# Half-head blocks with 64 KB rows in a decode attention kernel that streams K and V

## The chip, the cores and the metric

The kernel runs on one core of a Trainium2 chip. The metric is device time in microseconds (us), the median of several executions. All runs told here were classed as fast (no execution over 1.5% above the fastest of its kernel); executions of one kernel agree within about 0.3%, and medians of several of them closer, so differences of half a per cent can be told apart when kernels are timed in the same rounds on the same chip.

## The reference

One query token, 32 query heads, 8 K/V heads, 65536 keys, head size 128, all in bf16. Each K/V head serves four query heads.

```python
B, Hq, Hkv, Sq, Sk, D = 1, 32, 8, 1, 65536, 128
scores = jnp.einsum("bhqd,bhkd->bhqk", q, k) * D ** -0.5
p = softmax(scores, axis=-1)
return jnp.einsum("bhqk,bhkd->bhqd", p, v)
```

K and V are 134 MB each. Every byte is read once, so the kernel is a stream of 268.44 MB through the core.

## The kernel before

A K/V head is cut into C = 4 blocks of 16384 keys. A block is 4 MB of K and 4 MB of V. Partition p takes 128 keys that lie next to each other, so one partition's row of a transfer is 32 KB. There are three K buffers and two V buffers.

```python
T = 128                 # keys per partition in a block
TG = 16                 # keys per partition in a group: one transpose
U = 2                   # score units in a block, one PSUM bank each
NK, NV = 3, 2           # K and V buffers
NKT = 4                 # buffers of transposed K
...
def load_k(i):
    if i >= NK:
        sp.wait_ge(tr_s, (i - NK + 1) * G)      # block i-3 is transposed
    ...
    sp.dma_start(kbuf[i % NK][:, :], src(kf, i)).then_inc(k_in[i % NK], 16)

def load_v(i):
    if i >= NV:
        sp.wait_ge(pv_s, i - NV + 1)            # block i-2 is multiplied
    ...
for j in range(N + LAG):                        # LAG = 5: V trails K by a head
    if j < N:
        load_k(j)
    if j >= LAG:
        load_v(j - LAG)
```

SyncE issues the loads in this order. VectorE (DVE) transposes each group of K in 32x32 blocks. TensorE (PE) multiplies the transposed K with the spread query into PSUM (`scores`). ScalarE (ACT) copies the scores to SBUF in 32x64 pieces, 16 of them per unit. When all four blocks of a head have scores, GpSimd takes the maximum over partitions, ACT takes exponentials, and PE multiplies them with V (`values`), four columns per key row. The last V block is loaded in small pieces to shorten the end.

```python
def move(u):                                    # ACT: one unit of scores, PSUM to SBUF
    ...
    for x in range(A):
        for a in range(A):                      # A = 4: 16 small copies
            ins = ac.activation(to[a * S4:(a + 1) * S4, x, :, :],
                                fr[x * S4:(x + 1) * S4, a, :, :], AF.Copy)
```

## Time and profile before

| before | value |
|---|---|
| time | 638.81 us (median of 4) |
| profiled span, first to last instruction | 636.8 us |
| bytes read / mean rate over the span | 268.47 MB / 422 GB/s |
| busiest engine | DVE, 53% |

These are lines of the page of before: the span, the busy time of each engine, then the span in 40 slices with the busy tenths of the DMA engines and their rate, the packet counts, and the chain of work that ended last. q1 is the queue on which K and V come, q8 and q14 bring instructions.

```profile
span 636.8 us, 20414 instructions
PE 325.1 (51%) x8197; PEld 294.2 (46%) x8197; DVE 334.7 (53%) x379; ACT 290.8 (46%) x1291; POOL 7.2 (1%) x25
...
DMA  9999999999999999999999999999999999999995
GB/s 369 436 422 441 431 428 428 430 431 430 434 434 439 430 427 427 430 432 434 431 434 436 432 427 428 430 430 435 420 430 432 422 428 418 434 429 385 389 423 246
...
q1 hardware_dynamic: 10656, 268.44, 98.6%
q8 instruction: 5, 0.08, 0.1%
q10 hardware_dynamic: 368, 0.04, 0.0%
q14 instruction: 13, 0.11, 0.0%
...
DMA 66%; DVE 20%; PE 10%; issue 2%; ACT 1%; SPq 1%; ACTq 0%
```

The DMA engines are busy in every slice until the last; no compute engine is above 53%. The kernel waits for its bytes.

The windows view of before, by stage (start and end, length, busy time and instructions of five engines, clock, DMA share, GB/s), shows the weak place at the end:

```profile
30.00:300.00 270.00, 141.87 (x3418) 126.61 (x3419) 161.64 (x173) 138.19 (x620) 2.77 (x7) 1.00 1.00 431
300.00:560.00 260.00, 131.88 (x3454) 120.97 (x3450) 140.16 (x157) 117.73 (x525) 2.40 (x6) 1.00 1.00 428
560.00:600.00 40.00, 22.88 (x640) 21.24 (x639) 15.85 (x23) 21.89 (x96) 0.82 (x2) 1.00 0.99 408
```

The trace also lists every DMA packet with its start, duration and size. One packet of the K/V queue is one partition's row. The median durations of before are:

| row | 2 KB | 4 KB | 8 KB | 16 KB | 32 KB |
|---|---|---|---|---|---|
| ns | 84 | 159 | 309 | 611 | 1213 to 1215 |

They lie on a straight line: about 9 ns, plus 27.2 GB/s per engine, which is 435 GB/s on 16 engines. The Trainium skill ("DMA: Bandwidth & Descriptors", Where 436 GB/s comes from) gives the same figure, 435.2 GB/s, as the ceiling of the ports on the SBUF side, and this trace agrees. All the bytes at 435 GB/s on 16 engines take 617.1 us.

### The profile page before, as it was taken

How to read it: one execution, taken by the hardware profiler on the slowest of the kernel's cores; microseconds unless marked ns; L12 is line 12 of the kernel's file. 1: busy time of each engine (PE TensorE's matmuls, PEld its weight loads, DVE VectorE, ACT ScalarE, POOL GpSimd, SP SyncE). 2: the span in 40 equal slices, each digit the busy share in tenths (PEclk: the TensorE clock that was granted, in tenths of full speed). 3: DMA queues.
4: the chain of work that ended last, by engine and by line, in shares of the span. 5: the costliest groups of instructions: out<-in, count | busy, mean ns of one | idle time of the engine just before them, and what ended most of it. 6: DMA issues, size and time to landing. Idle time of an engine off the chain costs nothing.

```text
span 636.8 us, 20414 instructions
## 1 busy us (share of the span) xinstructions
PE 325.1 (51%) x8197; PEld 294.2 (46%) x8197; DVE 334.7 (53%) x379; ACT 290.8 (46%) x1291; POOL 7.2 (1%) x25
## 2 busy tenths in 40 slices
PE   2466764345653456634466434665345654385346
PEld 1355554335552345533455433554334553375335
DVE  5599865445664446654466534566344664482000
ACT  1466854355433554335553345533355434466120
POOL 0000000000000000000000000000000000000000
DMA  9999999999999999999999999999999999999995
GB/s 369 436 422 441 431 428 428 430 431 430 434 434 439 430 427 427 430 432 434 431 434 436 432 427 428 430 430 435 420 430 432 422 428 418 434 429 385 389 423 246
DMA packets 11042, 268.67 MB, mean 422 GB/s; under 512 B 1552, under 2 KB 1552, under 8 KB 2192
## 3 DMA queue, kind: packets, MB, share of 16 engines
q1 hardware_dynamic: 10656, 268.44, 98.6%
q8 instruction: 5, 0.08, 0.1%
q10 hardware_dynamic: 368, 0.04, 0.0%
q14 instruction: 13, 0.11, 0.0%
HBM read 268.47 MB, written 0.01 MB: 422 GB/s over the span
## 4 chain that ended last, share of the span: by engine, by line
DMA 66%; DVE 20%; PE 10%; issue 2%; ACT 1%; SPq 1%; ACTq 0%
DMA kbuf<-in_k_dram 59%; DVE ktb L278 18%; DMA vbuf<-in_v_dram 7%; PE qkb L178 5%; PE acc L189 4%; DVE hpart L286 2%; ACT scs L371 1%; SPq L135 1%; PE row L240 0%; SPq L125 0%; SPq L138 0%; PE row L246 0%; ACT olast L408 0%; DVE hmax L293 0%; PE acc L235 0%
## 5 line engine op out<-in xcount | busy, mean ns | idle before, releaser
L278 DVE STREAM_TRANSPOSE ktb<-kbuf 128x1024 int32<-128x1024 int32 x256 | 298.5, 1214 | 220.3 <-DMA kbuf<-in_k_dram 219.9
L178 PE MATMUL qkb<-qblk,ktb 128*128 x4096 | 224.6, 178 | 278.2 <-DVE ktb L278 268.1
L371 ACT ACTIVATE scs<-qkb 32x64 f32<-32x64 f32 x1024 | 219.5, 214 | 297.8 <-PE qkb L178 286.6
L178 PEld LDWEIGHTS qkb<-qblk,ktb 128*128 128x128 bf16 x4096 | 187.2, 105 | 305.3 <-issue 287.1
L189 PE MATMUL acc<-pts,vbuf 128*128 128x4 bf16 x4080 | 142.3, 166 | 31.3 <-DMA vbuf<-in_v_dram 29.9
L189 PEld LDWEIGHTS acc<-pts,vbuf 128*128 128x128 bf16 x4080 | 128.0, 104 | 34.5 <-DMA vbuf<-in_v_dram 29.4
L388 ACT ACTIVATE pts<-scs,negb 128x128 bf16<-128x128 f32 x128 | 66.9, 570 | 28.5 <-PE acc L189 27.7
L286 DVE TENSOR_REDUCE hpart<-scs 128x4 f32<-128x256 f32 x64 | 36.4, 569 | 5.8 <-ACT scs L371 5.8
L388 ACT ACTIVATION_READ_ACCUMULATOR pts<-scs,negb 128x1 f32 x128 | 23.9, 187 | 0.0
L309 DVE TENSOR_TENSOR o<-acc,o 128x4 f32<-128x4 f32 x8 | 1.3, 162 | 38.0 <-PE acc L189 25.1
L306 DVE COPY o<-acc 128x4 f32<-128x4 f32 x8 | 1.3, 161 | 27.8 <-PE acc L189 27.8
L163 POOL PARTITION_ALL_REDUCE hmaxa<-hmax x8 | 3.0, 371 | 574.4 <-DVE hmax L293 574.4
L408 ACT ACTIVATE olast<-row,rrow 4x128 bf16<-4x128 f32 x1 | 0.4, 358 | 15.4 <-PE row L240 15.4
L167 POOL PARTITION_ALL_REDUCE lsum<-rsum x7 | 3.6, 511 | 0.9 <-ACT pts L388 0.9
L360 ACT ACT_TABLE_LOAD x1 | 1.3, 1283 | 2.7 <-issue 2.7
L240 PE MATMUL row<-vbuf,pts 128*4 128x128 bf16 x16 | 2.1, 308 | 0.0
L293 DVE TENSOR_REDUCE hmax<-hpart 128x4 f32<-128x32 f32 x8 | 1.7, 210 | 0.3
L240 PEld LDWEIGHTS row<-vbuf,pts 128*4 128x4 bf16 x16 | 1.6, 122 | 0.2
L379 ACT ACTIVATE negb<-hmaxa 128x4 f32<-128x4 f32 x8 | 1.6, 203 | 0.2
L256 DVE STREAM_TRANSPOSE qt<-q 128x64 int32<-128x64 int32 x1 | 0.2, 245 | 2.5 <-DMA q<-in_q_dram 2.5
L317 DVE RECIPROCAL recip<-lhead 128x4 f32<-128x4 f32 x7 | 1.2, 178 | 0.2
L321 DVE TENSOR_TENSOR oT<-o,recip 128x4 bf16<-128x4 f32 x7 | 1.1, 163 | 0.2
(24 smaller groups left out, 6.9 us busy)
## 6 DMA issues: line engine op xcount, KB each, us to landing
vbuf<-in_v_dram SPq DMA_DIRECT2D x31, 4096.0 KB, 17.4
kbuf<-in_k_dram SPq DMA_DIRECT2D x30, 4096.0 KB, 26.8
kbuf<-in_k_dram SPq DMA_DIRECT2D x5, 1024.0 KB, 22.2
kbuf<-in_k_dram SPq DMA_DIRECT2D x1, 2048.0 KB, 11.2
vbuf<-in_v_dram SPq DMA_DIRECT2D x1, 2048.0 KB, 10.3
kbuf<-in_k_dram SPq DMA_DIRECT2D x2, 512.0 KB, 4.3
vbuf<-in_v_dram SPq DMA_DIRECT2D x1, 1024.0 KB, 12.5
vbuf<-in_v_dram SPq DMA_DIRECT2D x1, 512.0 KB, 13.2
```

The costliest lines, as they stand in the source:

```text
L135: sp.dma_start(vbuf[i % NV][:, :], src(vf, i)).then_inc(v_in[i % NV], 16)
L163: g.partition_all_reduce(hmaxa[:, hs], hmax[:, hs], P, bass.bass_isa.ReduceOp.max).then_inc(hma_s, 1)
L167: g.partition_all_reduce(lsum[:, ps], rsum[:, ps], P, bass.bass_isa.ReduceOp.add).then_inc(ls_s, 1)
L178: ins = pe.matmul(qkb[(e * U + g // GU) % NQ][:, at:at + A * R], lhsT=kt[:, be // NE, be % NE, n * P:(n + 1) * P], rhs=qblk[:, bass.ds(col ...
L189: ins = pe.matmul(acc[:, 0:R], lhsT=vbuf[e][:, t * D:(t + 1) * D], rhs=pts[e][:, t * R:(t + 1) * R], start=e == 0 and t == 0, stop=e == E ...
L240: ins = pe.matmul(row[0:R, 0:D], lhsT=pts[E - 1][:, t * R:(t + 1) * R], rhs=vbuf[E - 1][:, t * D:(t + 1) * D], start=t == T - TG, stop=t = ...
L278: dv.transpose(to.rearrange("p (b t j) -> p b t j", b=NB, t=TG), fr.rearrange("p (t b i) -> p b t i", b=NB, t=TG),).then_inc(tr_s, 1)
L286: dv.tensor_reduce(hp[:, h % 2, c, :], scs[h % 2][:, c * W:(c + 1) * W].rearrange("p (n g) -> p g n", g=R), AX.X, ALU.max,).then_inc(mx_s, 1)
L293: dv.tensor_reduce(hmax[:, h * R:(h + 1) * R], hp[:, h % 2, :, :].rearrange("p u g -> p g u"), AX.X, ALU.max,).then_inc(hm_s, 1)
L371: ins = ac.activation(to[a * S4:(a + 1) * S4, x, :, :], fr[x * S4:(x + 1) * S4, a, :, :], AF.Copy)
L379: ac.activation(negb[:, hs], hmaxa[:, hs], AF.Copy, scale=-scale).then_inc(nb_s, 1)
L388: ac.activation(pv[:, g_, :], sv[:, g_, :], AF.Exp, bias=negb[:, col], scale=scale, accum_out=rsum[:, i * R + g_:i * R + g_ + 1],).then_in ...
```

## The change

The intent is fewer and longer rows. A head is now cut into C = 2 blocks of 32768 keys; a partition's row is 64 KB and a transfer is 8 MB. Two K buffers and one V buffer of 8 MB take 192 KB of each SBUF partition, where the five buffers of before took 160; to make room, the buffers of transposed K fall from four to two, and the small tensors are packed into one. The score buffer now holds one block instead of two heads, so the softmax runs with a maximum that is corrected at the second block: the first block's sums and outputs are multiplied by exp(first maximum - total maximum). The last two V blocks are loaded in halves, each as soon as PE has done the same half of the block before.

```diff
-T = 128
+T = 256
-U = 2
+U = 4
-NK, NV = 3, 2
-NKT = 4
+NK = 2
+NKT = 2
-KLAST = (32, 32, 32, 32)
+KLAST = (64, 64, 64, 64)
+HALVED = 2
...
         def load_v(i):
-            if i >= NV:
-                sp.wait_ge(pv_s, i - NV + 1)
+            if i < N - HALVED:
+                if i >= 1:
+                    sp.wait_ge(pv_s, 2 * i)
+                load(vbuf, vf, i, 0, T, v_in)
+                return
+            sp.wait_ge(pv_s, 2 * i - 1)
+            load(vbuf, vf, i, 0, TH, va_in)
+            sp.wait_ge(pv_s, 2 * i)
...
-        for j in range(N + LAG):
+        load_k(0)
+        for j in range(1, N + 1):
             if j < N:
                 load_k(j)
-            if j >= LAG:
-                load_v(j - LAG)
+            load_v(j - 1)
...
+        def weigh(h):
+            ...
+            dv.tensor_tensor(o2, o1, wgt, ALU.mult).then_inc(ow_s, 1)
+            ...
         def exponent(i):
...
+            if b:
+                ac.activation(wgt, dif, AF.Exp, scale=scale).then_inc(wg_s, 1)
```

PE's loop now does all 16 groups of `scores` of block j and then all `values` of block j-1, where before it did them group by group in turn. The waits cut from `weigh` and `exponent` above are in the kernel.

## The prediction

> **What bounds the kernel now.** The transfers. The page's DMA row is 9 in every slice but the last; the HBM line gives 422 GB/s over the 636.8 us span. No engine is over 53% busy (DVE 334.7 us). The chain of waits is 66% DMA. Windows by stage: 431 GB/s in 30–300 us, 428 in 300–560, but 408 in 560–600.
>
> In the trace's list of DMA packets one packet is one partition's row; median times are 84, 159, 309, 611, 1213 ns for 2, 4, 8, 16, 32 KB: a straight line, about 8.5 ns fixed plus 27.2 GB/s per engine, 435 GB/s on 16. The Trainium skill ("DMA: Bandwidth & Descriptors", Where 436 GB/s comes from) states the same ceiling, 435.2; this trace agrees. The bytes alone need 617 us. The other 20 us of the span (an estimate, from the packets): 2.75 before the first packet, 5.3 fixed packet cost (9472 rows x 9 ns / 16), 0.7 completions, 5 of packets slower than their median, 3.4 after the last packet, 3 of under-filled engines in the V-only tail, where a V load waits for PE to free one of two buffers.
>
> **What the change does.**
> - 5760 data rows instead of 9472, 45 transfers instead of 74. Saves 3712 x 9 / 16 = 2.1 us plus 0.3 for completions, if a 64 KB row is one packet; nothing if it is cut in two.
> - One K buffer, one V buffer and two of four transposed-K buffers go. A V load now waits for all value matmuls of the block before, which PE does after the next block's scores. From K_j landing (t = 0; an 8 MB transfer is 19.5 us): 16 transposes at 1.22 us (1.13 back to back, plus waits for two buffers) plus two maxima at 0.5: scores end near 22. V_{j-1} landed at 19.5; values, 256 x 34 ns = 8.7, end at 31; V_j is issued then, while K_{j+1} fills the engines to 39. Slack 8 us against 2.0 from an issue to its first packet: no bubble.
> - Exponentials (256 wide, under 1 us each) run near 31–36; the running maximum adds about six operations of 0.2 us per head. Off the critical path: DVE works 33 of 39 us per block.
> - Tail: DVE stands in `collect` for block 13 until 31 after K_14 landed, transposes block 15 until 54; values(14) follow, so V_15's first half is issued near 59, just after V_14 landed (58.5): one bubble of 2–3 us, in place of the 3 us lost now.
>
> **Predicted time.** 638.85 − 2.4 (packets) − 0.5 (tail) − 0.3 (fewer slow packets) = 635.7 us. Range 631 to 641. Faster by over 2%: 0.01 (bytes plus start and end alone are about 625). Within 2%: 0.93. Slower: 0.06.
>
> **What would show each step.** 64 KB packets of about 2419 ns and about 6480 packets on the K/V queue (10000 mean the rows are cut); middle slices of 431–434 GB/s; DVE still waiting for K several us per block; SyncE waiting for PE before V loads with K in flight; one dip below 400 GB/s where the last V starts.
>
> **What would make it wrong.** Bubbles in every block, if transposes, scores and values take over 37 us from K's landing (each lost us costs 15 in all). A 64 KB pitch slower in HBM: the same page (Latency and other measured facts) reports slower copies at large power-of-two pitches, such as 2 MiB; no run here shows it. More slow packets.

## More of the kernel before

The costliest groups of instructions of before (line, engine, operation, tiles, count, then busy us, mean ns, and the idle time before them with its cause):

```profile
L278 DVE STREAM_TRANSPOSE ktb<-kbuf 128x1024 int32<-128x1024 int32 x256 | 298.5, 1214 | 220.3 <-DMA kbuf<-in_k_dram 219.9
...
L371 ACT ACTIVATE scs<-qkb 32x64 f32<-32x64 f32 x1024 | 219.5, 214 | 297.8 <-PE qkb L178 286.6
```

DVE stands idle for 220 us waiting for K.

## The result, and the profile after

| | before | after |
|---|---|---|
| time, median of 4 | 638.81 us | 636.12 us |
| span of the profiled run | 636.8 us | 634.0 us |
| data rows / transfers of K and V | 9472 / 74 | 5760 / 45 |
| first packet to last packet, from the first instruction | 1.73 to 632.40 us | 1.72 to 629.72 us |

The ratio of after to before is 0.9957, 95% interval 0.9939 to 0.9974. A ratio is the mean time of one kernel's fast runs over that of the other's of the same rounds, so it is not quite the ratio of the medians in the tables. The predicted time was 635.7 us, in a range of 631 to 641.

The same parts of the page of after:

```profile
span 634.0 us, 18764 instructions
PE 271.7 (43%) x8197; PEld 245.2 (39%) x8197; DVE 341.0 (54%) x411; ACT 276.2 (44%) x1179; POOL 10.3 (2%) x33
...
DMA  9999999999999999999999999999999999999995
GB/s 365 429 450 418 443 430 435 438 426 438 422 447 426 438 426 435 438 422 447 418 455 418 442 431 426 442 422 443 422 455 410 451 426 434 430 410 437 430 359 219
...
q1 hardware_dynamic: 6480, 268.44, 98.4%
q8 instruction: 5, 0.08, 0.1%
q14 instruction: 14, 0.11, 0.0%
...
DMA 48%; DVE 27%; PE 15%; another core or an unknown queue 9%; issue 1%; SPq 1%; POOL 0%; ACT 0%; ACTq 0%
```

The queue carries 6480 packets: 5760 rows and 45 x 16 completions, as predicted. A 64 KB row is one packet, median 2421 ns (the line gives 2419). The slices swing more because one packet is now 2.4 us; the windows view of after gives the rates that can be compared:

```profile
30.00:300.00 270.00, 116.23 (x3498) 104.54 (x3499) 153.48 (x178) 125.65 (x541) 3.90 (x10) 1.00 1.00 432
300.00:560.00 260.00, 110.02 (x3359) 99.59 (x3357) 137.73 (x163) 110.94 (x473) 3.90 (x10) 1.00 1.00 434
560.00:600.00 40.00, 22.18 (x658) 19.74 (x659) 31.80 (x38) 24.77 (x109) 0.80 (x2) 1.00 0.98 420
```

The groups of after that answer to those of before:

```profile
L284 DVE STREAM_TRANSPOSE ktb<-kbuf 128x1024 int32<-128x1024 int32 x256 | 295.8, 1213 | 161.2 <-DMA kbuf<-in_k_dram 158.2
L375 ACT ACTIVATE scs<-qkb 32x64 f32<-32x64 f32 x1024 | 220.5, 215 | 281.3 <-PE qkb L184 270.1
```

DVE still waits for K, 158 us, in every block. The timeline of after around a block in the middle (start, length, what):

```profile
433.81 10.38 DVE L284 STREAM_TRANSPOSE ktb<-kbuf 128x1024 int32<-128x1024 int32 x9 [10.91 <-DMA kbuf<-in_k_dram]
...
453.84 6.98 PE L195 MATMUL acc<-pts,vbuf 128*128 128x4 bf16 x256
...
460.85 0.33 SPq L119 DMA_DIRECT2D vbuf<-in_v_dram  x1
...
472.51 8.16 DVE L284 STREAM_TRANSPOSE ktb<-kbuf 128x1024 int32<-128x1024 int32 x7 [11.49 <-DMA kbuf<-in_k_dram]
```

K lands at 433.81, `values` of the block before end at 460.8, the next V is issued 27.0 us after the landing, and the next K lands 38.7 us after it. The issue comes 11.7 us before the K transfer ahead of it is done, so the engines do not run dry. This is the main wait that the change could have lost to, and it costs nothing.

So far the prediction stands. Two things did not fit. First, the tail of after still has under-filled slices; in slices of 2 us they are 355 and 280 GB/s at 602 to 606 us and 298 twice at 614 to 618 us. Second, the packets that are slower than their median are not spread evenly, and most follow an 8 KB packet on the instruction queue. The experiments take the row length first and then these two.

A correction for what follows: the prediction and the first texts place packets on an axis that begins 1.0 to 1.3 us before the first instruction. In this section and in all tables the axis begins at the first instruction, as in the profile's views. The prediction's "2.75 before the first packet" and "3.4 after the last packet" are 1.73 and 4.4 us on it, with the same sum, and its "2.0 from an issue to its first packet" is about 1.0 us (before: issue at 577.93, first packet at 578.91).

### The profile page after: what moved, and what is told of

The parts are those of the page before. It is cut to its first block, busy times and chain, and to the rows that moved or that the text cites. A ratio compares the mean times of both kernels' runs of the same rounds, so it can differ in the third digit from the quotient of the medians.

```text
span 634.0 us, 18764 instructions
## 1 busy us (share of the span) xinstructions
PE 271.7 (43%) x8197; PEld 245.2 (39%) x8197; DVE 341.0 (54%) x411; ACT 276.2 (44%) x1179; POOL 10.3 (2%) x33
## 3 DMA queue, kind: packets, MB, share of 16 engines
q1 hardware_dynamic: 6480, 268.44, 98.4%
## 4 chain that ended last, share of the span: by engine, by line
DMA 48%; DVE 27%; PE 15%; another core or an unknown queue 9%; issue 1%; SPq 1%; POOL 0%; ACT 0%; ACTq 0%
DMA kbuf<-in_k_dram 30%; DVE ktb L284 25%; DMA vbuf<-in_v_dram 17%; PE acc L195 13%; PE qkb L184 2%; DVE small L291 1%; SPq L119 1%; PE row L248 0%; POOL small L165 0%; PE row L254 0%; DVE small L335 0%; ACT ktb L408 0%; DVE small L317 0%; DVE small L313 0%
## 5 line engine op out<-in xcount | busy, mean ns | idle before, releaser
L284 DVE STREAM_TRANSPOSE ktb<-kbuf 128x1024 int32<-128x1024 int32 x256 | 295.8, 1213 | 161.2 <-DMA kbuf<-in_k_dram 158.2
L184 PE MATMUL qkb<-qblk,ktb 128*128 x4096 | 157.3, 176 | 343.0 <-DVE ktb L284 330.3
L184 PEld LDWEIGHTS qkb<-qblk,ktb 128*128 128x128 bf16 x4096 | 132.9, 105 | 367.2 <-issue 199.0
L195 PE MATMUL acc<-pts,vbuf 128*128 128x4 bf16 x4080 | 112.0, 166 | 17.2 <-DMA vbuf<-in_v_dram 16.7
L195 PEld LDWEIGHTS acc<-pts,vbuf 128*128 128x128 bf16 x4080 | 110.4, 104 | 18.9 <-DMA vbuf<-in_v_dram 15.1
L291 DVE TENSOR_REDUCE small<-scs 128x4 f32<-128x256 f32 x64 | 38.0, 593 | 61.4 <-ACT scs L375 61.4
L392 ACT ACTIVATE pts<-scs,small 128x256 bf16<-128x256 f32 x64 | 48.9, 852 | 34.8 <-PE acc L195 34.8
L160 POOL PARTITION_ALL_REDUCE small<-small x16 | 6.0, 372 | 574.8 <-DVE small L302 574.8
L392 ACT ACTIVATION_READ_ACCUMULATOR pts<-scs,small 128x1 f32 x64 | 13.6, 212 | 0.0
L381 ACT ACTIVATE small<-small 128x4 f32<-128x4 f32 x16 | 3.3, 205 | 21.8 <-POOL small L160 21.8
L313 DVE TENSOR_TENSOR small<-small 128x4 f32<-128x4 f32 x8 | 1.3, 163 | 18.1 <-PE acc L195 18.1
L307 DVE TENSOR_TENSOR small<-small 128x4 f32<-128x4 f32 x8 | 1.3, 164 | 4.0 <-POOL small L160 4.0
L165 POOL PARTITION_ALL_REDUCE small<-small x7 | 3.0, 432 | 18.5 <-DVE small L317 18.5
L315 DVE TENSOR_TENSOR small<-small 128x4 f32<-128x4 f32 x8 | 1.3, 156 | 2.7 <-ACT pts L392 2.7
```

Source lines behind the costliest of these rows:

```text
L160: g.partition_all_reduce(mtot if b else mfirst, hmax[:, b * R:(b + 1) * R], P, bass.bass_isa.ReduceOp.max,).then_inc(hma_s, 1)
L165: g.partition_all_reduce(lsum, rhead, P, bass.bass_isa.ReduceOp.add).then_inc(ls_s, 1)
L184: ins = pe.matmul(qkb[g // GU][:, at:at + A * R], lhsT=kt[:, be // NE, be % NE, n * P:(n + 1) * P], rhs=qblk[:, bass.ds(qcols[be], A * R)] ...
L195: ins = pe.matmul(acc[:, 0:R], lhsT=vbuf[:, t * D:(t + 1) * D], rhs=pts[:, t * R:(t + 1) * R], start=t == 0, stop=t == T - 1,)
L284: dv.transpose(to.rearrange("p (b t j) -> p b t j", b=NB, t=TG), fr.rearrange("p (t b i) -> p b t i", b=NB, t=TG),).then_inc(tr_s, 1)
L291: dv.tensor_reduce(hp[j % C][:, u * R:(u + 1) * R], scs[:, u * W:(u + 1) * W].rearrange("p (n g) -> p g n", g=R), AX.X, ALU.max,).then_inc ...
```

## The experiments

Twelve kernels ran; all gave correct outputs. The kernel before was timed in the same rounds each time; its medians were 638.5 to 638.8 us. before_wide and the three busy runs ran on another chip than the rest, so times of different rounds are best compared through the ratio.

| run | time, us | ratio to before, 95% interval |
|---|---|---|
| rows_32k | 638.63 | 0.9996 (0.9983 to 1.001) |
| rows_16k | 642.58 | 1.0058 (1.0044 to 1.0072) |
| quarter_tail | 636.03 | 0.9958 (0.9944 to 0.9972) |
| late_collect | 636.23 | 0.9959 (0.9945 to 0.9973) |
| act_nops | 639.20 | 1.001 (0.9996 to 1.0023) |
| dve_nops | 637.59 | 0.9984 (0.9971 to 0.9998) |
| wide | 633.11 | 0.9917 (0.9903 to 0.9931) |
| wide_quarter | 633.26 | 0.9918 (0.9904 to 0.9931) |
| before_wide | 635.38 | 0.9952 (0.9938 to 0.9965) |
| busy_256 | 652.85 | 1.0212 (1.0195 to 1.0228) |
| busy_384 | 738.17 | 1.156 (1.1542 to 1.1578) |
| busy_mid | 642.44 | 1.0062 (1.005 to 1.0074) |

### Is the gain the fixed cost of a packet? rows_32k and rows_16k

The changed kernel, with each whole 8 MB transfer cut into CUT = 2 or 4 transfers of shorter rows. Nothing else changes.

```diff
-                load(kbuf[i % NK], kf, i, 0, T, k_in[i % NK])
+                for c in range(CUT):
+                    load(kbuf[i % NK], kf, i, c * T // CUT, (c + 1) * T // CUT, k_in[i % NK])
...
-            dv.wait_ge(k_in[j % NK], 16 * (j // NK + (j % NK > 0)))
+            dv.wait_ge(k_in[j % NK], 16 * CUT * (j // NK + (j % NK > 0)))
```

V is cut in the same way.

> The changed kernel with each of its 28 whole 8 MB transfers cut into two of 32 KB rows; buffers, waits and softmax as changed. Theory A (the gain is the fixed 8.5 to 9 ns of a packet): 3584 more rows and 28 more transfers cost 3584 x 9 / 16 + 28 x 9 = 2.3 us, so 638.4 us, median 32 KB packet 1213 ns, about 10500 packets on the queue. Rival B (the gain comes from the rest of the change: other waits, fewer slow packets): the time stays within 0.3 us of the changed kernel, 636.1 us.

> The same with four transfers of 16 KB rows. Theory A: three times as much, 6.0 + 0.8 = 6.8 us, so 642.9 us, median 16 KB packet 611 ns. Rival B: still 636 to 637 us.

Measured: 638.63 and 642.58 us, against 638.4 and 642.9 expected for theory A. The median packets were 1218 and 613 ns. The queue counts follow: 6480 packets in after, these in rows_32k and then rows_16k (lines of their pages).

```profile
q1 hardware_dynamic: 10512, 268.44, 98.5%
```

```profile
q1 hardware_dynamic: 18576, 268.44, 98.7%
```

With 32 KB rows the changed kernel takes the time of the kernel before. So the whole gain is the row length, and the rest of the change, with fewer buffers, another order of loads and another softmax, is neutral in sum. Rival B fell. (A cut adds transfers as well as rows, in a fixed proportion, so these runs do not part the cost of the two; the packet durations do: two rows of 32 KB take 2 x 1213 = 2426 ns, one of 64 KB 2418 to 2421.)

### Does the tail cost anything? quarter_tail and late_collect

In after, the tail runs like this (timeline; the first half of V_14 lands, PE multiplies it, only then may the first half of V_15 be issued):

```profile
599.94 3.57 PE L195 MATMUL acc<-pts,vbuf 128*128 128x4 bf16 x128 [0.83 <-DMA vbuf<-in_v_dram]
...
609.64 3.57 PE L195 MATMUL acc<-pts,vbuf 128*128 128x4 bf16 x128 [6.12 <-DMA vbuf<-in_v_dram]
```

PE ends the first half at 603.5. Yet the fastest DMA engine has nothing left to do from 602.96, where its part of V_14 ends. quarter_tail loads the last two V blocks in quarters, so that more is in flight:

```diff
-            sp.wait_ge(pv_s, 2 * i - 1)
-            load(vbuf, vf, i, 0, TH, va_in)
-            sp.wait_ge(pv_s, 2 * i)
+            for c in range(4):
+                sp.wait_ge(pv_s, 4 * (i - 1) + c + 1)
+                if i < N - 1 or c < 2:
+                    load(vbuf, vf, i, c * TQ, (c + 1) * TQ, vq_in[c])
+                    continue
```

late_collect keeps the halves and moves only DVE's collection of block 13 into the middle of block 15's transposes:

```diff
+                if j == N - 1 and g == G // 2 - 1:
+                    collect(N - 3)
...
-            if j >= 1:
+            if j >= 1 and j != N - 2:
                 collect(j - 1)
```

> The changed kernel with the last two V blocks loaded in quarters instead of halves, each issued as soon as PE has done the same quarter of the block before. Theory C (the tail starves because with halves the loop of [...]values 3.6, issue to first packet 2.1, plus 2 to 3 us spread between the 16 DMA engines, is longer than the 9.7 us a half takes): the loop shrinks to 6 + spread against 14.5 us of transfers in flight, both dips (273 and 331 GB/s near 604 to 608 us, 227 near 616) go, and the time falls by 2 to 2.8 us to 633.3 to 634.1 us. Rival D (the tail waits for DVE, which stands in the collection of block 13 before it transposes block 15, as the prediction had it): the first quarter of the last V goes out about 2.7 us earlier at best, the first dip shrinks, the second stays, gain about 1 us or less.

> The changed kernel with only the collection of block 13 moved from before to the middle of block 15's transposes, so that DVE starts on block 15 several us earlier; V in halves as changed. Theory C: no change (within 0.3 us of 636.1), because the first half of V_14 lands 0.8 us after PE is ready for it and stays the limit. Rival D: the dip near 604 us goes, 634 to 635 us.

Measured: 636.03 and 636.23 us, no gain from either. late_collect speaks against the prediction's reason for the dip (DVE standing in `collect`). quarter_tail is the surprise: it did what it should to the transfers and nothing to the time. In slices of 2 us the rate stays at 420 GB/s or more until 622 us; both dips are gone. But the last packet ends at 629.87 us, as in after (629.72). The rate only falls earlier: 339, 133, 43 and 24 GB/s in the four slices from 622 us. Most of the 16 DMA engines are done by about 624 us and wait for one.

Theory C thus described the dips rightly and their cost wrongly. (On the corrected axis its loop is 0.5 us from the last packet of a landing to PE's start, 3.6 of values, 1.0 from the issue to the first packet, and a spread of 6.2 us, 593.25 to 599.44, on the first half of V_14.) The fast engines were idle in the tail, but the last engine was not: it ended the halves of V_14 at 599.44 and 609.14 us, and the first half of V_15 had been issued at 603.55.

### One DMA engine sets the pace

Every engine writes one 4-byte completion packet per transfer, so the 16 completions of a transfer show when the first and the last engine were done with it. On transfers of after (the first row is a 4 MB piece of the first block, the others are whole; times in us):

| the first engine ended a transfer at | last engine | spread | instruction fetches of 8 KB since the row above |
|---|---|---|---|
| 22.18 | 24.50 | 2.33 | none |
| 41.50 | 44.86 | 3.36 | 36.7 (309 ns); also two of 16 KB at 39.2 and 39.5 |
| 351.10 | 354.57 | 3.47 | six, at 73.3 to 293.4 |
| 370.45 | 374.60 | 4.15 | 366.7 (309 ns) |
| 409.15 | 413.31 | 4.16 | none |
| 428.50 | 433.33 | 4.83 | 425.4 (309 ns), 428.4 (325 ns) |
| 467.20 | 472.04 | 4.84 | none |
| 486.55 | 492.07 | 5.52 | 489.0 (309 ns) |
| 544.60 | 550.11 | 5.51 | none |

The spread grows in steps of 0.67 to 0.69 us, and a step falls where an 8 KB packet of 309 ns stands on q14. The packet list shows the cost of one: at 489.0 us the fetch takes 309 ns on an engine, and the 64 KB row after it takes 2798 ns in place of 2421. That is 0.31 + 0.38 = 0.69 us. The Trainium skill ("DMA: Bandwidth & Descriptors", Queues, rings and completion order) says that row 14 of the queues is the runtime's own, for refills among others; these packets fit that. Nine fetches of 309 to 318 ns come, 51 to 76 us apart, and one more of 707 ns in the tail, at 617.8 us. The trace records 1226 ACT instructions, waits included (the expectations below count 1292); at 64 bytes each (the skill's "Runtime: NRT & Kernel Launch", Instruction fetch mechanics, counts 256 instructions to 16 KiB) 8 KB are 128 of them, which makes about 10 fetches, an estimate that act_nops checks below. A rarer kind of 325 ns, followed by a row of 3080 ns (1.0 us together), comes four times and would be DVE's, with 461 instructions recorded.

The packets carry no engine number. But on one engine a packet starts 3 to 4 ns before the recorded end of the last one, so the packets can be chained, which is a reconstruction and not a record. In it all nine fetches of the first kind lie on one engine and all four of 325 ns on another. The first of these engines lags 0.75 us behind the fastest near 61 us, 3.47 near 296 us and 5.52 near 492 us. That is why the fetches from 73 to 293 us hardly moved the spread: until then a third engine was last, 3.39 us behind, and the engine with the 309 ns fetches had yet to catch up with it.

This gives theory E: one DMA engine brings ACT's instructions besides its share of K and V, falls behind by 0.69 us at each fetch, and every landing waits for it. It predicts that the time follows the number of ACT instructions, though ACT is only 44% busy.

act_nops and dve_nops add 512 instructions that only step an unused semaphore, on ACT or on DVE:

```diff
                 move(j, u)
+                for _ in range(8):
+                    ac.nop().then_inc(idle_s, 1)
```

```diff
                 transpose(j, g)
+                for _ in range(2):
+                    dv.nop().then_inc(idle_s, 1)
```

wide goes the other way. It makes a score unit fill a whole PSUM bank, 512 columns, which halves the number of score copies; wide_quarter adds the quarters of quarter_tail:

```diff
-U = 4
+U = 2
```

> The changed kernel with 512 more ScalarE instructions that do nothing but step an unused semaphore (8 after each group of 16 score copies). Theory E (after quarter_tail: the time is set by one of the 16 DMA engines, the one that also brings ScalarE's instructions, 8 KB for every 128 of them; each such fetch holds its rows up by about 0.31 + 0.38 = 0.69 us, 10 times in a run, and the spread between first and last engine at the end of a transfer grows from 3.4 to 5.5 us in the trace of after): 4 more fetches, the last engine 2.7 us later, 638.8 us. Rival F (the mean rate of the 16 engines sets the time): 4 x 0.69 / 16 = 0.2 us, 636.3 us.

> The changed kernel with 512 more VectorE instructions of the same kind (2 after each transpose). VectorE's fetches fall on another DMA engine, about 0.325 + 0.66 = 1.0 us each, and that engine is some 3.4 us behind the first at the end. Theory E: 4 more fetches bring it to about 7.4 us, just behind ScalarE's engine at 6.9, so 636.1 to 637.0 us. Rival G (more instructions of any engine cost the same): as act_nops, 638.8 us. Rival F: 636.4 us.

> The changed kernel with score units of 512 columns instead of 256 (U = 2): half the score copies, so 748 ScalarE instructions instead of 1292 and 5 to 6 fetches in place of 10. Theory E: ScalarE's DMA engine gains 4.5 x 0.69 = 3.1 us and then lies level with VectorE's, so 633.0 to 633.6 us. Rival F: 0.2 us, 635.9 us. Work on ScalarE falls by some 50 us in all, off the critical path under both.

> wide together with the last two V blocks in quarters (quarter_tail). Theory E: the dips of the tail cost at most what they push beyond the slowest engine, which now ends earlier; 632.5 to 633.4 us, at most 0.7 us better than wide. Rival F: the sum of both, 633.1 us from an unchanged 635.9 less 2.8 for the tail; but quarter_tail alone, which gained 0.1 us, already speaks against it.

Measured: act_nops 639.20, dve_nops 637.59, wide 633.11, wide_quarter 633.26 us. The instruction queue of act_nops, and then the engines and that queue of wide:

```profile
q14 instruction: 18, 0.15, 0.1%
```

```profile
PE 271.0 (43%) x8197; PEld 244.7 (39%) x8197; DVE 338.2 (54%) x379; ACT 193.2 (31%) x667; POOL 10.2 (2%) x33
...
q14 instruction: 9, 0.07, 0.0%
```

The kinds of fetch show whose they are. In after 10 are of the first kind (with the one of 707 ns) and 4 of 325 ns; act_nops has 14 and 4, dve_nops 10 and 8 (325 or 333 ns), wide 6 and 3. So 512 instructions are four fetches, on ACT or on DVE.

Four more fetches of ACT cost about 3.1 us (636.12 to 639.20, from different rounds; 2.7 expected), and the spread near 545 us grows from 5.51 to 8.47, again in steps of 0.69 behind each fetch. Five fetches fewer, four of ACT's and one of DVE's, save about 3.0 us, and the spread is 3.52. dve_nops costs 1.5 us, less than the same number on ACT as expected, but more than the 0.0 to 0.9 expected: I had taken DVE's engine to be 3.4 us behind at the end, and it still had its fetch near 600 us before it. Rival F, that the mean rate of all engines counts, fell with all three (0.2 us expected each time), and rival G fell with dve_nops. wide_quarter is not faster than wide: the tail is free there too.

Part of wide's gain may be something else. The spread near 42 us is 2.20 in it and 3.36 in after, because the 16 KB fetches of q8 near 39 us came at the same time in after (1391 and 2205 ns) and one by one in wide (about 1.0 us each). Near 545 us, two engines of wide are level, 3.52 and 3.22 us behind the first, so fewer ACT fetches alone are not likely to help further.

If theory E holds, the kernel before had the same burden, and its gain is open to it without the change. before_wide makes only the score units of before wider:

```diff
-U = 2
+U = 1
...
-NQ = 4
+NQ = 2
```

> The kernel before with score units of 512 columns (U = 1, two score banks in place of four) and nothing of the change: 770 ScalarE instructions instead of 1314, so 6 fetches in place of 10 or 11. Theory E: the DMA engine that brings ScalarE's instructions also sets the pace of the kernel before (spread 4.7 us near 548 us in its trace, second slowest engine 2.1), so it gains about 2.6 us before the second engine takes over: 635.7 to 636.5 us, as much as the whole change. Rival F (mean rate): 638.5 us.

Measured: 635.38 us, ratio 0.9952, a little below the 635.7 to 636.5 expected. Two edited constants in the kernel before give as much as the whole change.

With the last engine as the one to account for, each run's last packet is a sum: the first packet, 617.1 us for a sixteenth of the bytes, 9 ns for each packet of one engine (8 rows and one completion per transfer), and a remainder, the time by which this engine is late.

| run | first packet | bytes | fixed | late | last packet |
|---|---|---|---|---|---|
| before | 1.73 | 617.1 | 6.0 | 7.6 | 632.40 |
| after | 1.72 | 617.1 | 3.6 | 7.3 | 629.72 |
| rows_32k | 1.75 | 617.1 | 5.9 | 7.7 | 632.42 |
| rows_16k | 1.75 | 617.1 | 10.5 | 7.5 | 636.76 |
| quarter_tail | 1.74 | 617.1 | 3.9 | 7.2 | 629.87 |
| late_collect | 1.74 | 617.1 | 3.6 | 7.7 | 630.13 |
| act_nops | 1.72 | 617.1 | 3.6 | 10.6 | 633.05 |
| dve_nops | 1.73 | 617.1 | 3.6 | 9.2 | 631.61 |
| wide | 1.73 | 617.1 | 3.6 | 4.5 | 626.97 |
| wide_quarter | 1.73 | 617.1 | 3.9 | 4.3 | 627.01 |
| before_wide | 1.73 | 617.1 | 6.0 | 4.3 | 629.05 |

Two terms describe eleven kernels: the number of packets, and the lateness of one engine, which is 7.2 to 7.7 us in the six that have about 1200 to 1300 ACT instructions and no added DVE ones, whatever their buffers and tails. Lateness is what remains in the sum, so the table does not show its cause; the runs that add and remove instructions do. The change moved the first term by 2.35 us and the second hardly. The sequencer fetches are a measured part of the lateness (10 x 0.69 us would be 6.9, an estimate); which other delays make up the rest for each engine was not taken apart.

### How much slack has a V load? busy_256, busy_384, busy_mid

The prediction gave a V load 8 us of room. These runs put idle matmuls in front of `values`, so that V is issued later.

```diff
             with pe.If_eq(skip, 0):
+                for _ in range(BUSY):
+                    pe.matmul(row[:, 0:R], lhsT=qblk[:, 0:P], rhs=qblk[:, 0:R], start=True, stop=True)
                 pe.wait_ge(co_s, it - 1)
```

> The changed kernel with 256 idle matmuls of 28 ns put before each block's value matmuls: every V load is issued 7.1 us later. From the trace of after, a V load is issued 27.2 us after its block's K has landed (550.6 to 577.8), its first packets follow 1 to 1.5 us later, and the slowest DMA engine ends the K transfer before it 38.3 us after that landing: slack 9.6 us for the slowest engine, 4.1 for the fastest. Theory E (slowest engine paces): no loss, within 0.5 us of 636.1 us, while the fast engines wait for the issue and the spread between first and last engine falls from 5.5 to about 2.5 us. As the prediction on record had it (values end at 31, room until 37): 1.1 us lost in each of 14 blocks, about 651 us.

> The same with 384 idle matmuls, 10.7 us. Theory E with the slack of 9.6 us: 1 to 2.3 us lost in each of 14 blocks (DVE, which waits for the values, is late for the next K as well), 650 to 668 us. As the prediction on record had it: 4.7 us in each block, about 702 us.

Measured: 652.85 and 738.17 us. On time alone busy_256 looks like the prediction (651), but the trace says otherwise. In the middle of the run (timeline of busy_256):

```profile
403.25 10.39 DVE L287 STREAM_TRANSPOSE ktb<-kbuf 128x1024 int32<-128x1024 int32 x9 [5.52 <-DMA kbuf<-in_k_dram]
...
436.92 0.33 SPq L120 DMA_DIRECT2D vbuf<-in_v_dram  x1
...
442.77 10.39 DVE L287 STREAM_TRANSPOSE ktb<-kbuf 128x1024 int32<-128x1024 int32 x9 [4.49 <-DMA kbuf<-in_k_dram]
```

V is issued 33.7 us after the landing and 5.9 us before the next, and between 90 and 610 us no stretch of 4 us has more than 4.8 us of idle time summed over the 16 engines. The loss lies at two places: near 80 to 89 us (gaps of 5.4 to 8.9 us on the engines) and in the tail near 615 to 627 us (7.6 to 12.1 us). At the first, PE also stood for its own instructions:

```profile
75.73 0.54 PE L229 MATMUL row<-qblk 128*128 128x4 bf16 x14 [3.87 <-issue]
...
83.16 3.55 PE L196 MATMUL acc<-pts,vbuf 128*128 128x4 bf16 x127 [3.78 <-issue]
```

From K_3's landing to K_14's, 11 blocks on, busy_256 takes 429.0 us and after 427.9, so in the middle the later issue costs about 0.1 us a block.

busy_384 is no measurement of slack at all: its instructions were fetched again and again, 73 blocks of 16 KB on q8 (5 in after), and PE stood up to 4 us inside the idle matmuls. Its expectation missed by 70 us for that reason. busy_mid therefore uses few, wide idle matmuls and is meant to leave out the first blocks and the tail:

```diff
+            with pe.If_eq(edge, 0):
+                for _ in range(BUSY):
+                    pe.matmul(row[:, :], lhsT=qblk[:, 0:P], rhs=qblk[:, :], start=True, stop=True)
             with pe.If_eq(skip, 0):
```

> The changed kernel with 32 idle matmuls of 512 columns (about 7 us together, an estimate from 37 ns for 16 columns in the trace of after and the work growing with the columns) before the value matmuls of blocks 2 to 13 only, so that neither the first V loads nor the tail is delayed, and with few enough PE instructions to need no further fetches. From busy_256: its loss lies at two places (idle DMA engines near 81 to 90 us, where PE also stood for its own instructions, and near 616 to 626 us in the tail), none in the blocks between. If the slack of a middle block is over 7 us: 636.1 us within 0.5. If it were the 6 us of the prediction on record (31 to 37): about 1 us lost in each of 12 blocks, 648 us.

Measured: 642.44 us, between the 636.1 expected for a slack over 7 us and the 648 for one of 6. Again the place of the loss decides. In a middle block:

```profile
239.51 10.38 DVE L290 STREAM_TRANSPOSE ktb<-kbuf 128x1024 int32<-128x1024 int32 x9 [2.85 <-DMA kbuf<-in_k_dram]
...
259.33 8.96 PE L231 MATMUL row<-qblk 128*128 128x512 bf16 x32
...
274.83 0.33 SPq L120 DMA_DIRECT2D vbuf<-in_v_dram  x1
...
278.21 10.38 DVE L290 STREAM_TRANSPOSE ktb<-kbuf 128x1024 int32<-128x1024 int32 x9 [2.01 <-DMA kbuf<-in_k_dram]
...
318.31 10.43 DVE L290 STREAM_TRANSPOSE ktb<-kbuf 128x1024 int32<-128x1024 int32 x9 [5.15 <-DMA kbuf<-in_k_dram]
```

The idle matmuls took 9 us, and V was issued 35.3 us after the landing and 3.4 us before the next. The 38.7 us between these two landings say nothing of this V, since the K that landed at 278.21 was already in flight. Its effect is in the next period, which is 40.1 us (278.21 to 318.31) and 38.8 in after (277.54 to 316.33). No engine ran dry at this issue (no idle time between 240 and 282 us), but one 64 KB row that began at 277.6 us took 4045 ns. Rows of over 2500 ns where a late V begins come after every one of these issues, and in after at none. In all, from K_3's landing to K_14's, busy_mid takes 430.9 us and after 427.9: 3.0 us lost over ten such V loads, 0.3 us each.

The engines ran dry at two of the issues, by 15 engine-us near 158 us and 9 near 394. The first cost nothing: only the faster engines waited, the spread fell from 3.29 to 1.09 us, and the last engine ended the next K at 199.66 us, in after at 199.67.

The last packet ends 6.4 us later than in after (636.14 and 629.72), so the other 3.4 us are in the tail (timeline of busy_mid):

```profile
590.17 10.38 DVE L290 STREAM_TRANSPOSE ktb<-kbuf 128x1024 int32<-128x1024 int32 x9
...
610.46 6.98 PE L196 MATMUL acc<-pts,vbuf 128*128 128x4 bf16 x256 [0.32 <-issue]
```

The idle matmuls before the values of block 13 delay `collect` for that block, and DVE stands in it before it transposes block 15. So the transposes begin 11.1 us later than in after (579.10), the values of block 14 begin at 610.46 in place of 599.94, and all engines run out of work, the first at 608.8 and the last at 612.4 us. The edit was meant to leave the tail alone and did not. The values themselves were not slower: 256 of them take 6.98 us, as in after, although the granted PE clock fell in this run (lines of its page; in all other runs told here the clock is 1.0):

```profile
PEclk9999999999575575756758556585765757558555
DMA  9999999999999999999999999999999999999966
```

So a V load in the middle of the run may be issued 6.6 us later (33.7) for about 0.1 us a block, and 8 to 9 us later (35.0 to 36.4) for about 0.3. No sharp limit was found; busy_384, which was to pass it, was spoiled. In the tail the slack is smaller (busy_256). For the first V loads busy_256 settles nothing: the one near 88 us was issued 15.6 us later than in after, not 7, as PE also stood for its instructions.

## Why the prediction was right or wrong

The time was right: 635.7 predicted, 636.12 measured. Of the 3.2 us of gain that it promised 2.7 came, the packet term with 2.4 of them; the tail term came to nothing, the third is too small to tell from noise, and the account of the 20 us beside the bytes was right in sum by luck.

- **The fixed packet cost, -2.4 us: right.** The last engine's fixed cost fell by 2.35 us (6.0 to 3.6), a 64 KB row is one packet of 2421 ns (2419 predicted), and cutting the rows gives the time back (rows_32k, 638.63) and on beyond it in proportion (rows_16k). A pitch of 64 KB between rows in HBM is not slower.
- **No bubble in a block: right, with a size off.** The prediction had `values` ending 31 us after K's landing; it is 27.0, because they begin at 20.0 and not 22, and a value matmul takes 27 ns (6.98 us for 256) and not 34. busy_256 delayed the issue to 33.7 us at a cost of about 0.1 us a block.
- **The softmax and the smaller buffers off the critical path: right.** rows_32k, which has them all, takes the time of before (the two were not tested apart).
- **The tail: the step that failed.** The prediction counted "3 of under-filled engines in the V-only tail" as part of the 636.8 us, and "one bubble of 2-3 us, in place of the 3 us lost now" as a gain of 0.5. It took an idle DMA engine for lost time. There were two dips, the issue came 53 us after K_14's landing instead of 59 (550.6 to 603.5), late_collect showed that `collect` does not set it, and quarter_tail showed that removing both dips is worth nothing.
- **"5 of packets slower than their median": right in amount, wrong in nature.** This was a mean over engines. Slow packets pile up on single engines, where the instruction fetches are, and the last engine is what counts. It was late by 7.6 us in before and 7.3 in after. These 7.6 stand in place of the prediction's 5 + 3 = 8, which is why a wrong account gave a right sum. That was luck.
- **"Fewer slow packets, -0.3 us":** the lateness fell by 0.3 us, which is too small to trust; it varies from 7.2 to 7.7 among kernels that should have the same.

The version that beats both kernels is wide, the changed kernel with U = 2: 633.11 us, ratio 0.9917 to before. It adds the two terms: 64 KB rows (2.4 us) and fewer ACT instructions (3.0 us).

## What to carry to other kernels

A transfer has landed when the slowest of the 16 DMA engines is done, so in a kernel bound by DMA look at the spread between first and last engine before you look at the mean rate: idle time of the fast engines cost nothing here. An engine's instruction count is a DMA cost even when the engine is half idle; fewer, larger instructions (one constant here) were worth 3.0 us, and doubling the row length 2.7. And a predicted time that comes out right does not show that its terms are right: only the run that removed the tail's bubble showed that the bubble had never cost anything.

## What the Trainium skill lacked or had wrong

- "Runtime: NRT & Kernel Launch" (Instruction fetch mechanics) says that an engine's instructions are refilled in 16 KiB blocks, 256 instructions, and that crossing a block is mostly hidden. In these traces only q8 shows 16 KB packets; q14 brings 8 KB at a time, and the number follows ACT's and DVE's instructions (512 more give 4 more packets). Whatever it costs the engine that fetches, it is not hidden from the DMA engine that carries it: 0.69 us each for the 309 ns kind, 1.0 us for the 325 ns kind. 512 ACT instructions more or fewer moved the time by 3 us in 636.
- The same section says that a long kernel is streamed from memory at little cost, but also that a taken branch to a page that is not loaded stalls the engine. It gives no size for the stall. busy_384, whose loop has 384 more matmuls, fetched 73 blocks, and PE stood up to 4 us at a time.
- "DMA: Bandwidth & Descriptors" gives no fixed time per packet for large rows. Here it is about 9 ns from 2 KB to 64 KB rows, worth 2.4 us in 636 between 32 KB and 64 KB rows, and 64 KB is still one packet. Its ceiling of 435.2 GB/s agrees (27.2 GB/s per engine).
- The same page (Latency and other measured facts) reports slower copies at large power-of-two row pitches, measured from 512 KiB up. It has no figure for 64 KB, where this case shows no loss: 2421 ns per row against 2419 from the line.
- No page that I read says how far one engine's lag grows through a stream: in after it reached 5.5 us near 545 us and was not made up. It shrank where the faster engines ran out of work, from 3.29 to 1.09 us in busy_mid near 158 us.
